# Products with zeros behind the attention products of slots 11 to 17

## The chip, the cores and the metric

The program runs on one NeuronCore of a Trainium2 chip. A core has five engines with queues of their own, which work at the same time and wait for each other by semaphores: TensorE (PE in the rows; its weight loads stand there as PEld), VectorE (DVE), ScalarE (ACT), GpSimd (POOL) and SyncE (SP, which here only issues transfers). TensorE writes into eight banks of PSUM; VectorE and ScalarE read them. The metric is the time of one execution on the device in microseconds (us); lower is better.

## The reference

Three stages, each on the result of the one before. For the attention there are 2 batches of 8 heads, 768 positions and a width of 64; a query sees the keys less than 16 positions away and 24 block summaries.

```python
scores_l = scale * np.matmul(q, k.transpose(0, 1, 3, 2))        # kept where |i - j| < 16
scores_s = scale * np.einsum('bhsd,bhnd->bhsn', q, k_sum) + np.log(block)
a = softmax(concatenate([scores_l_m, scores_s]))
attn_out = a @ concatenate([v, v_sum])
...
expert_idx = argmax(x_normed @ emb_normed.T / tau)               # 1536 rows, 8 experts, one each
out[mask] = gate * (relu(x[mask] @ w1[e]) @ w2[e])
...
h = x @ w_in                                                     # 512 -> 2048
return (h * cos(h)) @ w_out
```

## The kernel before, in words

**Attention in slots.** Two heads of one batch are a pair; there are 8 pairs, and each is done in two halves, so there are 16 half-pairs. The loop `for i in range(NH + 2)` runs over 18 slots, i = 0 to 17, and works as a pipeline of three half-pairs. Slot i does, in this order on TensorE:

- transposes for the pair to come: `pk` (line 205) in even slots, `pq` (line 178) in odd ones;
- the scores of half-pair i, `ps` (line 263; 12 products);
- the output products of half-pair i-2, `po` (`attn_av`, line 307; 12 products of a 120-row `aT` with the values and a column of ones), into a PSUM tile named `po` of which there is one;
- the transposes of half-pair i-1, `pa` (line 291; 6).

VectorE adds the mask to the scores (line 272), takes the maxima (279), and turns `po` into output rows (lines 313, 314, 316: add, reciprocal, multiply). ScalarE copies `pa` to `aT` (line 296) and takes the exponentials (284). So from one slot to the next there is a chain: `po`, then `pa` on TensorE, then the copy `aT` on ScalarE, then the next slot's `po`. That `po` also needs line 316 of the slot before, which frees the one tile. Slots 16 and 17 have no scores and no preparation.

**What else stands in the last slots.** The string `PLAN` places pieces of the routing of batch 0 in the slots 4 to 17: norms, logits, the pick of the expert, positions, and from slot 13 the scattering of its rows to DRAM by GpSimd (line 542). When the rows have landed, window 0 of the experts is loaded from there (line 751), scaled by its gate (764), transposed (`px`, line 778, behind slot 17's `po`), copied by ScalarE (780) and VectorE (781), and the first products of the experts (`h`, line 720) begin.

**The first expert window.** It forms `h`, then `y` (both line 720, 128 rows); in between stand turns of `h` (`pz`, line 851), the two halves of the transposes of window 1 (`px`, line 787, copied in lines 789 and 790), and the routing of batch 1 (transposes `pxr`, line 374, copied in 377; sums of squares in line 406). The weights of all windows are split into two parts by ScalarE (629) and VectorE (630). Windows 1 to 6 follow, then the dense stage; every product there is line 720 too.

**What sets the order.** The attention's own code is under `manual_schedule()`: it stays in the order in which it is written. What is written later, the expert stage and the routing of batch 1, is placed by the framework's scheduler, by its own estimate of when each engine is free; it can put such an instruction between those of the last slots. On the chip each engine then works through its list in that order.

**Zeros.** `still` is a tile of zeros [128, 256] in SBUF. `keep_warm` (line 1010) multiplies it with itself into an unused bank, three times in the first 18 us (line 1013).

Of the kernel before, what the change touches and what calls it, by code (L numbers as in the profile page):

```python
# [21 lines left out]
P = 128  # L22
# [29 lines left out]
ON_VECTOR = "e2 k4 k6 k8 k12 k14 x2 x3 x5"  # L52

EARLY = (2, 12)
NWMAX = 24
TT = 384
TWO_PI = 2.0 * math.pi
# [47 lines left out]
def fused_kernel(ctx, tc, q, k, v, emb, tau, w1, w2, w_in, w_out, consts, out):  # L105
    nc = tc.nc
# [57 lines left out]
    def shuffle(raw, n, scale, ap, eng, r=None):  # L164

        if r is None:
            r = ap.tile([P, QJ, 2, D], F32, tag="shuf", name="shuf", bufs=1)
        r = r[0:n]
        eng.tensor_scalar(
            r.rearrange("p j h d -> p h j d"), raw.rearrange("p h (j d) -> p h j d", d=D),  # L170
            scale, 1.0, op0=ALU.mult, op1=ALU.mult,
        )
        return r
# [52 lines left out]
    def prep_v1(bf, ap, eng):  # L226
        v4 = bf["vn"].rearrange("p h (j d) -> p h j d", d=D)
        va = ap.tile([QP, 2, 4, D], F32, tag="va", name="va", bufs=1)
        eng.tensor_tensor(va, v4[:, :, 0:4, :], v4[:, :, 4:8, :], op=ALU.add)
        eng.tensor_tensor(va[:, :, 0:2, :], va[:, :, 0:2, :], va[:, :, 2:4, :], op=ALU.add)  # L230
        eng.tensor_tensor(va[:, :, 0, :], va[:, :, 0, :], va[:, :, 1, :], op=ALU.add)
        return va
# [63 lines left out]
            nc.scalar.activation(aT[0:KC], pa[0:KC], AF.Copy)  # L296
        return aT

    def attn_av(g, half, aT, bf, xb, ps_s, ap):

        vw = bf["vw"][half]
        pb = ps_s.tile([P, 512], F32, tag="po", name="po")
        po = pb[:, 0:NU * (D + 1)].rearrange("p (u h d) -> p u h d", u=NU // 2, h=2)
        for u in range(NU):
            m = 64 * (u % 2)
            for hh in range(2):
                nc.tensor.matmul(
                    po[m:m + 64, u // 2, hh, :],
                    lhsT=aT[0:KC, (3 * hh + u // 2) * P + m:(3 * hh + u // 2) * P + m + 64], rhs=vw[0:KC, hh, u, :],
                    start=True, stop=True,  # L310
                )
        rs = ap.tile([P, NU // 2, 2], F32, tag="rs", name="rs")
        nc.vector.tensor_scalar(rs, po[:, :, :, D], 1e-9, None, op0=ALU.add)
        nc.vector.reciprocal(rs, rs)
        j0 = half * (NU // 2)
        nc.vector.tensor_tensor(
            xb[:, j0:j0 + NU // 2, 2 * g * D:2 * (g + 1) * D].rearrange(
                "p u (h d) -> p u h d", h=2
            ),
            po[:, :, :, 0:D], rs.unsqueeze(3).to_broadcast([P, NU // 2, 2, D]), op=ALU.mult,  # L320
        )
# [670 lines left out]
    with ExitStack() as actx:  # L992
        actx.enter_context(tc.manual_schedule())
        ap1 = actx.enter_context(tc.tile_pool(name="ap1", bufs=1))
        ap = actx.enter_context(tc.tile_pool(name="ap", bufs=2))
        ps_t = actx.enter_context(tc.tile_pool(name="ps_t", bufs=1, space=PSUM))
        ps_s = actx.enter_context(tc.tile_pool(name="ps_s", bufs=1, space=PSUM))
# [9 lines left out]
        still = ap1.tile([P, 2 * P], F32, name="still")  # L1007
# [10 lines left out]
        sets = []  # L1018
# [29 lines left out]
        def q_room():  # L1048
            r = xp.tile([P, 2 * ROW], F32, tag="xw", name="qr", bufs=3)
            return r[:, 0:2 * QJ * D].rearrange("p (j h d) -> p j h d", j=QJ, h=2)  # L1050
# [29 lines left out]
        xbs = []  # L1080
        x0p = actx.enter_context(tc.tile_pool(name="x0p", bufs=1, side="right"))
        for b in range(B):
            if b == 0:
                xb = x0p.tile([P, NU, ROW], F32, name="xb0")
            else:
                xb = big[:, 0:NU * ROW].rearrange("p (u r) -> p u r", u=NU)
# [4 lines left out]
        def moe_start():  # L1091
            for i in range(3):
                expert_slots(slots, wtis[0], i)
            slots.load(4)
            yield
            xws.append(load_x0())
            yield
            slots.load(8)
            for i in range(1, 3):
                xws.append(load_x(wtis[0], i, xp, 3))  # L1100
            yield
            for n in range(12):
                slots.convert(n + 1)
                yield
# [8 lines left out]
        ss, aTs = {}, {}  # L1113
# [3 lines left out]
        start = moe_start()  # L1117
# [23 lines left out]
        for item in PLAN.split(";"):  # L1141
            where, *names = item.split()
            todo = plan.setdefault((int(where[:-1]), where[-1]), [])
            for name in names:
                name, _, times = name.partition("*")
                todo += [gens[name]] * int(times or 1)

        def at(i, place):
            for piece in plan.get((i, place), ()):
                next(piece, None)  # L1150
# [7 lines left out]
        for i in range(NH + 2):  # L1158
            def prep_qv():
                nonlocal qs, va  # L1160
                qs = shuffle(raw["qn"], QP, SCALE, ap, nc.gpsimd, q_room())
                va = prep_v1(raw, ap, nc.vector if f"v{i}" in on_vector else nc.gpsimd)
                if p + 2 < NPR:
                    load_raw(*pairs[p + 2], raw, "qv")

            p, odd = divmod(i, 2)
            if i == 3:
                nc.sync.dma_start(cst[:, P:], consts[:, P:C_VIND])
                next(setup)
                for b, xb in enumerate(xbs):  # L1170
                    nc.gpsimd.memset(xb[:, :, DM:ROW], 0.0)
                    nc.gpsimd.tensor_copy(
                        xb[:, :, DM:DM + 1],
                        csa[:, C_TOK - C_VIND + b * NU:C_TOK - C_VIND + (b + 1) * NU].unsqueeze(2),
                    )
            if i == 7:
                zt = xp.tile([P, ROW], F32, tag="junk", name="zt")
                nc.gpsimd.memset(zt[:, 0:DM], 0.0)
                nc.gpsimd.memset(zt[:, DM:ROW], 1e6)
                for r0 in (S, NTOK):  # L1180
                    nc.sync.dma_start(
                        xs[r0:r0 + WT].rearrange("(a p) d -> p a d", p=P),
                        zt.unsqueeze(1).to_broadcast([P, WT // P, ROW]),
                    )
            at(i, "0")
            nx = sets[(p + 1) % 2] if p + 1 < NPR else None
            if nx is not None and not odd and i > 2:
                pk = ps_t.tile([P, QJ, P], F32, tag="tr", name="pk")
                prep_k(
                    nx, kr, [pk], ap, nc.vector if f"k{i}" in on_vector else nc.gpsimd,  # L1190
                    f"e{i}" in on_vector,
                )
            elif nx is not None and odd and i > 1:
                prep_q(nx, qs, ps_t, nc.scalar)
            at(i, "p")
            if i in EARLY:
                prep_qv()
            if i < NH:
                s, nmx, vsm = attn_scores(
                    odd, sets[p % 2], ps_s, ap, va if nx is not None and odd and i > 1 else None  # L1200
                )
                ss[i] = s
            at(i, "s")
            if i == 0:
                prep_v3(sets[0], means_v(va))
                va = prep_v1(raw, ap, nc.gpsimd)
                load_raw(*pairs[2], raw, "v")
                load_vw(*pairs[1], 0, sets[1]["vw"][0])
            if i == 1:
                prep_q(nx, qs1, ps_t, nc.scalar)  # L1210
            if i == 2:
                pk = ps_t.tile([P, QJ, P], F32, tag="tr", name="pk")
                prep_k(nx, kr, [pk], ap, nc.gpsimd, f"e{i}" in on_vector)
            at(i, "c")
            if i >= 2:
                b, g = pairs[p - 1]
                attn_av(g, odd, aTs.pop(i - 2), sets[(p - 1) % 2], xbs[b], ps_s, ap)
                if p + 1 < NPR:
                    load_vw(*pairs[p + 1], odd, nx["vw"][odd])
            at(i, "h")  # L1220
            if 0 <= i - 1 < NH:
                aTs[i - 1] = attn_aT(ss.pop(i - 1), ps_a, ap, i)
            if i == 1:
                keep_warm(4, P, ps_s, "s")
            if i < NH:
                attn_exp(s, nmx)
            if nx is not None and not odd and i and i not in EARLY:
                prep_qv()
            if odd and p + 2 < NPR:
                kr = shuffle(raw["kn"], QP + 4, 1.0, ap, nc.vector if i == 1 else nc.gpsimd)  # L1230
                if p + 3 < NPR:
                    load_raw(*pairs[p + 3], raw, "k")
            if i == 1:
                vsm1 = means_v(va)
                load_vw(*pairs[1], 1, sets[1]["vw"][1])
            if i == 2:
                prep_v3(sets[1], vsm1)
            elif nx is not None and odd and i > 1:
                prep_v3(nx, vsm)
            at(i, "e")  # L1240
            if i == 0:
                prep_k(nx, kr, two_banks(), ap, nc.gpsimd)
# [119 lines left out]

    n_all = nc.values_load(wtis[1][0:1, 2:3], min_val=0, max_val=NWMAX)
    with tc.For_i(NSLOT, n_all, 1) as it, ExitStack() as lctx:
# [74 lines left out]
```

## Time and profile before

| | us |
|---|---|
| median of 3 runs | 539.42 (539.02 to 539.49) |
| profiled execution: time | 539.12 |
| profiled execution: span of the program | 537.3 |
| TensorE busy | 506.7 (94%) |
| VectorE busy | 404.3 (75%) |
| ScalarE busy | 304.0 (57%) |
| GpSimd busy | 107.6 (20%) |
| mean granted clock of TensorE | 0.984 of full speed |

The attention takes the first 96 us, the experts run from about 98 to 266 us, the dense stage from there. Busy shares are means over stages with different limits; the clock's mean of 0.984 comes from a start at half speed and one stretch in the attention. Times in rows are microseconds from the start of the span unless they are marked ns. TensorE's products of 32-bit numbers stand as two rows each (x24 for 12 products), transposes as one.

### The profile page before, as it was taken

The numbers are of one execution on the slowest core, as the hardware profiler recorded it, in microseconds if no ns is written. First come the engines' busy times: TensorE is split into PE (matmuls) and PEld (weight loads), VectorE is DVE, ScalarE is ACT, GpSimd is POOL, SyncE is SP. The second block draws the span as 40 slices with busy tenths as digits, with TensorE's granted clock in tenths as the row PEclk, the third lists the DMA queues.
The fourth block names the chain that finished last, engine by engine and source line by source line (L and its number), as shares of the span: only waits on it lengthen the run. The fifth ranks groups of instructions, "written<-read, shape, count | busy, mean of one in ns | idle before, by whom it ended". The sixth has DMA issues, their size and how long they took to land. (4 is left out here: it accounts for less than half of the span.)

```text
span 537.3 us, 10198 instructions
## 1 busy us (share of the span) xinstructions
PE 506.7 (94%) x3748; PEld 459.7 (86%) x3748; DVE 404.3 (75%) x834; ACT 304.0 (57%) x642; POOL 107.6 (20%) x134
## 2 busy tenths in 40 slices
PE   7879977899999999999999999999999999999993
PEld 6657656679999999999999999999999999999992
DVE  5689784898768688889779998976699765655562
ACT  2778865997656556566557675633364433333330
POOL 3787574751534000000000000000000000001222
PEclk9999986999999999999999999999999999999998
DMA  8999747787797566766304433220010000001111
GB/s 213 243 206 253 176 109 254 266 285 244 247 333 259 160 209 219 234 197 199 119 2 137 138 117 119 78 79 0 1 40 2 1 0 1 0 2 59 60 59 63
DMA packets 47688, 72.31 MB, mean 135 GB/s; under 512 B 21256, under 2 KB 21512, under 8 KB 47632
## 3 DMA queue, kind: packets, MB, share of 16 engines
q1 hardware_dynamic: 44800, 62.11, 39.6%
q0 software_dynamic: 2832, 9.49, 5.0%
q8 instruction: 31, 0.51, 0.4%
q14 instruction: 25, 0.20, 0.1%
HBM read 64.22 MB, written 7.37 MB: 133 GB/s over the span
## 5 line engine op out<-in xcount | busy, mean ns | idle before, releaser
L720 PE MATMUL po<-sl,gt 128*128 128x512 f32 x567 | 139.8, 391 | 0.0
L720 PEld LDWEIGHTS po<-sl,gt 128*128 128x128 f32 x567 | 105.5, 188 | 18.2
L720 PE MATMUL ph<-yT,sl 128*128 128x384 f32 x576 | 107.7, 336 | 0.0
L720 PEld LDWEIGHTS ph<-yT,sl 128*128 128x128 f32 x576 | 101.2, 188 | 3.7
L630 DVE TENSOR_TENSOR sl<-raw,sl 128x512 fp32r<-128x512 f32 x112 | 75.0, 706 | 11.3 <-ACT sl L629 10.9
L973 POOL DMA_INDIRECT out_dram<-acc,perm x12 | 12.0, 998 | 345.1 <-DVE acc L1349 342.6
L720 PE MATMUL py<-ht,sl 128*128 128x256 f32 x576 | 73.8, 284 | 0.0
L629 ACT ACTIVATE sl<-raw 128x512 fp32r<-128x512 f32 x112 | 63.5, 625 | 17.5 <-PE py L720 12.3
L720 PE MATMUL ph<-xT,sl 128*128 128x256 f32 x576 | 72.3, 282 | 1.0 <-DVE ht L816 1.0
L720 PEld LDWEIGHTS ph<-xT,sl 128*128 128x128 f32 x576 | 69.7, 188 | 2.4 <-DVE ht L816 1.4
L720 PEld LDWEIGHTS py<-ht,sl 128*128 128x128 f32 x576 | 70.4, 188 | 0.9 <-issue 0.6
L930 ACT ACTIVATE u<-u 128x384 f32<-128x384 f32 x64 | 33.6, 525 | 62.9 <-DVE u L929 62.8
L934 ACT ACTIVATE gt<-t 128x384 fp32r<-128x384 f32 x63 | 33.0, 524 | 31.3 <-DVE t L933 31.1
L926 ACT ACTIVATE t<-ph 128x384 f32<-128x384 f32 x64 | 31.3, 488 | 31.6 <-PE ph L720 31.2
L933 DVE TENSOR_TENSOR t<-ph,u 128x384 f32<-128x384 f32 (+1 forms) x66 | 35.8, 544 | 17.7 <-ACT u L930 17.5
L935 DVE TENSOR_TENSOR gt<-t,gt 128x384 fp32r<-128x384 f32 x63 | 35.1, 557 | 17.2 <-ACT gt L934 16.6
L928 DVE TENSOR_SCALAR u<-t 128x384 f32<-128x384 f32 x64 | 23.0, 359 | 27.7 <-ACT t L926 27.2
L929 DVE TENSOR_TENSOR u<-t,u 128x384 f32<-128x384 f32 x64 | 35.6, 557 | 1.1
L720 PE MATMUL ph<-yT,early 128*128 128x384 f32 x192 | 36.1, 338 | 0.2 <-DVE yT L1296 0.2
L720 PEld LDWEIGHTS ph<-yT,early 128*128 128x128 f32 x192 | 33.9, 188 | 1.7 <-DVE yT L1296 0.5
L284 ACT ACTIVATE s<-s,nmx 128x120 f32<-128x120 f32 x96 | 29.0, 385 | 2.6 <-DVE nmx L279 1.5
L815 ACT ACTIVATE ht<-ph 128x256 fp32r<-128x256 f32 x48 | 17.8, 378 | 15.9 <-PE ph L720 15.9
(189 smaller groups left out, 652.8 us busy)
## 6 DMA issues: line engine op xcount, KB each, us to landing
raw<-in_moe_w_dram SPq DMA_DIRECT2D x56, 512.0 KB, 4.1
raw<-in_moe_w_in_dram SPq DMA_DIRECT2D x16, 512.0 KB, 3.7
raw<-in_moe_w_out_dram SPq DMA_DIRECT2D x16, 512.0 KB
vw<-in_v_dram SPq DMA_DIRECT2D x32, 120.0 KB, 6.1
xw<-xs POOLq DMA_DIRECT2D x6, 516.0 KB
kn<-in_k_dram SPq DMA_DIRECT2D x8, 384.0 KB, 4.6
qn<-in_q_dram SPq DMA_DIRECT2D x8, 384.0 KB, 5.0
vn<-in_v_dram SPq DMA_DIRECT2D x8, 384.0 KB, 5.8
```

What stands on the lines that cost most here:

```text
L284: nc.scalar.activation(s[:, u, :], s[:, u, :], AF.Exp, bias=nmx[:, u:u + 1])
L629: nc.scalar.activation(sl[:, 0, c], r, AF.Copy)
L630: nc.vector.tensor_tensor(sl[:, 1, c], r, sl[:, 0, c].bitcast(F32), op=ALU.subtract)
L720: nc.tensor.matmul(acc, lhsT=lw(a), rhs=lx(c), start=(first and i == 0), stop=(last and i == 2))
L815: nc.scalar.activation(ht[:, 0], ph, AF.Relu)
L926: nc.scalar.activation(t, ph, AF.Copy, scale=1.0 / TWO_PI, bias=0.25)
L928: nc.vector.tensor_scalar(u, t, ROUND, -ROUND, op0=ALU.add, op1=ALU.add)
L929: nc.vector.tensor_tensor(u, t, u, op=ALU.subtract)
L930: nc.scalar.activation(u, u, AF.Sin, scale=TURN)
L933: nc.vector.tensor_tensor(g, ph[:, cs], u[:, cs], op=ALU.mult)
L934: nc.scalar.activation(gt[:, 0], g, AF.Copy)
L935: lo = nc.vector.tensor_tensor(gt[:, 1], g, gt[:, 0].bitcast(F32), op=ALU.subtract)
```

## The change

A table `FILL` gives the slots 11 to 17 a number of extra products. `attn_av` issues them behind its own twelve: zeros (128x128) times zeros (128x112), into columns 400 to 511 of the bank in which `po` uses the columns 0 to 389. Nobody reads these columns. All slots together get 34 such products.

```diff
+FILL = {11: 4, 12: 4, 13: 4, 14: 5, 15: 5, 16: 6, 17: 6}
...
-    def attn_av(g, half, aT, bf, xb, ps_s, ap):
+    def attn_av(g, half, aT, bf, xb, ps_s, ap, fill=0):
...
                     start=True, stop=True,
                 )
+
+        for _ in range(fill):
+            nc.tensor.matmul(
+                pb[:, 400:512], lhsT=still[:, 0:P], rhs=still[:, 0:112], start=True, stop=True
+            )
         rs = ap.tile([P, NU // 2, 2], F32, tag="rs", name="rs")
...
-                attn_av(g, odd, aTs.pop(i - 2), sets[(p - 1) % 2], xbs[b], ps_s, ap)
+                attn_av(
+                    g, odd, aTs.pop(i - 2), sets[(p - 1) % 2], xbs[b], ps_s, ap, FILL.get(i, 0)
+                )
```

In the built program line 313 of VectorE (320 after), the first reader of `po`, waits for the last instruction that wrote the tile: before, the last of the twelve products; now, in the slots 11 to 17, the last product with zeros.

The change also moves what the scheduler places. TensorE from slot 16 to the first expert products, before (lines of before):

```order
L307 MATMUL po<-vw_129,aT 64x65 x12
L291 MATMUL pa<-cst,s 120x128 x6
L374 MATMUL pxr<-cst,big 128x128
L307 MATMUL po<-vw_130,aT 64x65 x12
L778 MATMUL px<-cst,xw 128x128 x4
L374 MATMUL pxr<-cst,big 128x128 x4
L720 MATMUL h<-sl,xT 128x512 x18
```

and now (lines of the changed kernel, which are 2 higher up to line 311 and 7 higher behind the new loop at 315; 381 is 374, 785 is 778):

```order
L309 MATMUL po<-vw_129,aT 64x65 x12
L316 MATMUL po<-still 128x112 x6
L293 MATMUL pa<-cst,s 120x128 x6
L381 MATMUL pxr<-cst,big 128x128
L309 MATMUL po<-vw_130,aT 64x65 x12
L316 MATMUL po<-still 128x112 x6
L785 MATMUL px<-cst,xw 128x128 x4
L381 MATMUL pxr<-cst,big 128x128 x4
L727 MATMUL h<-sl,xT 128x512 x18
```

Here only the products with zeros are new: they stand between `po` and `pa`, and in slot 17 between `po` and the transposes of the first expert window.

ScalarE at the same place, before (`sl` is a weight tile, `junk` takes the squares for batch 1's norms, `hr` is the first half of `h`):

```order
L629 ACTIVATE sl<-raw 128x512
L377 ACTIVATE big<-pxr 128x512
L406 ACTIVATE junk,nm_91<-big 128x512
L780 ACTIVATE xT<-px 128x4x128
L629 ACTIVATE sl<-raw 128x512 x7
L377 ACTIVATE big<-pxr 128x512
L844 ACTIVATE hr<-h 128x512
L406 ACTIVATE junk,nm_91<-big 128x512
```

and now (636 is 629, 384 is 377, 413 is 406, 787 is 780, 851 is 844):

```order
L636 ACTIVATE sl<-raw 128x512
L384 ACTIVATE big<-pxr 128x512
L413 ACTIVATE junk,nm_91<-big 128x512 x3
L787 ACTIVATE xT<-px 128x4x128
L636 ACTIVATE sl<-raw 128x512 x7
L384 ACTIVATE big<-pxr 128x512
L851 ACTIVATE hr<-h 128x512
```

Two more sums of squares have moved in front of the copy of the first window's transposes.

TensorE in the `y` products of the first window, before (`px` of line 787 are the transposes of window 1):

```order
L720 MATMUL y<-sl,ht 128x512 x2
L787 MATMUL px<-cst,xw 128x128 x3
L720 MATMUL y<-sl,ht 128x512 x6
L787 MATMUL px<-cst,xw 128x128
L374 MATMUL pxr<-cst,big 128x128
L851 MATMUL pz<-cst,hr 128x128 x4
L720 MATMUL y<-sl,ht 128x512 x6
L787 MATMUL px<-cst,xw 128x128 x4
L720 MATMUL y<-sl,ht 128x512 x6
L374 MATMUL pxr<-cst,big 128x128 x2
L720 MATMUL y<-sl,ht 128x512 x4
L720 MATMUL ph<-xT,sl 128x256 x18
```

and now (727 is 720, 794 is 787, 858 is 851):

```order
L727 MATMUL y<-sl,ht 128x512 x8
L794 MATMUL px<-cst,xw 128x128
L858 MATMUL pz<-cst,hr 128x128 x4
L727 MATMUL y<-sl,ht 128x512 x4
L794 MATMUL px<-cst,xw 128x128 x3
L727 MATMUL y<-sl,ht 128x512 x12
L794 MATMUL px<-cst,xw 128x128 x4
L381 MATMUL pxr<-cst,big 128x128 x4
L727 MATMUL ph<-xT,sl 128x256 x3
L858 MATMUL pz<-cst,yr 128x128 x3
L727 MATMUL ph<-xT,sl 128x256 x17
```

The second half of window 1's transposes stood ten `y` products ahead of window 1's first products (`ph`, which read them); it now stands behind the last `y` product, directly ahead of `ph`.

## Rows read from the trace of the kernel before

**Rows 1.** The page, part 2: clock granted to TensorE in 40 slices of 13.4 us, tenths.

```profile
PEclk9999986999999999999999999999999999999998
```

**Rows 2.** Windows: length, busy us (instructions) of PE, PEld, DVE, ACT, POOL; clock; DMA share; GB/s.

```profile
52.00:55.00 3.00, 2.45 (x38) 2.14 (x38) 2.87 (x6) 2.73 (x7) 0.00 (x0) 1.00 1.02 191
...
76.00:77.00 1.00, 0.00 (x0) 0.00 (x0) 0.93 (x6) 1.00 (x5) 0.63 (x1) 0.50 0.00 0
89.00:90.00 1.00, 1.00 (x27) 0.95 (x24) 0.74 (x1) 1.00 (x5) 0.58 (x1) 0.71 0.05 20
...
160.00:170.00 10.00, 10.00 (x87) 10.00 (x86) 8.12 (x13) 7.05 (x15) 3.90 (x5) 1.00 0.82 281
```

**Rows 3.** Timeline of PE, 15 to 18 us: start, length, instruction; the last use of zeros.

```profile
16.30 1.10 PE L1013 MATMUL pw<-still 128*128 128x128 f32 x8
```

**Rows 4.** Timeline of PE, slots 12 and 13; in brackets idle time before, and its end.

```profile
70.27 0.97 PE L307 MATMUL po<-vw,aT 120*64 120x65 f32 x24 [0.96 <-ACT aT L296]
...
73.08 0.85 PE L178 MATMUL pq<-cst,qr 96*128 96x96 f32 x8 [0.78 <-ACT kb L196]
...
77.17 1.59 PE L307 MATMUL po<-vw,aT 120*64 120x65 f32 x24 [2.13 <-ACT s L284]
```

**Rows 5.** Timeline of PE, slot 14 from its middle to the first expert product.

```profile
85.10 1.15 PE L307 MATMUL po<-vw,aT 120*64 120x65 f32 x13 [0.46 <-issue]
86.18 1.54 PE L291 MATMUL pa<-cst,s 128*120 128x128 f32 x6
87.64 1.48 PE L263 MATMUL ps<-kb,qT 64*64 64x120 f32 x24
89.05 1.20 PE L307 MATMUL po<-vw,aT 120*64 120x65 f32 x24
...
92.25 0.94 PE L307 MATMUL po<-vw,aT 120*64 120x65 f32 x24 [1.09 <-ACT s L284]
93.12 0.87 PE L291 MATMUL pa<-cst,s 128*120 128x128 f32 x6
...
94.94 0.94 PE L307 MATMUL po<-vw,aT 120*64 120x65 f32 x24 [0.34 <-issue]
...
97.98 4.81 PE L720 MATMUL h<-sl,xT 128*128 128x512 f32 x18 [1.08 <-DVE xT L781]
```

**Rows 6.** Timeline of all engines in the same stretch: VectorE, GpSimd and ScalarE.

```profile
85.36 0.91 DVE L272 TENSOR_TENSOR s<-ps,csa 128x720 f32<-128x720 f32 x1 [3.70 <-remote]
...
89.42 1.65 POOL L248 TENSOR_SCALAR vw<-vsm 24x768 f32<-24x768 f32 x2 [5.42 <-ACT s L284]
...
91.09 0.81 ACT L296 ACTIVATE aT<-pa 120x768 f32<-120x768 f32 x1 [0.82 <-PE pa L291]
...
94.03 0.81 ACT L296 ACTIVATE aT<-pa 120x768 f32<-120x768 f32 x1 [0.42 <-PE pa L291]
...
95.73 0.63 ACT L406 ACTIVATE junk<-big 128x512 f32<-128x512 f32 x1
...
96.55 0.60 ACT L780 ACTIVATE xT<-px 128x512 fp32r<-128x512 f32 x1
...
97.23 0.69 DVE L781 TENSOR_TENSOR xT<-px,xT 128x512 fp32r<-128x512 f32 x1 [0.26 <-ACT xT L780]
```

**Rows 7.** Timeline, the second half of window 1's transposes, to window 1's first products.

```profile
109.07 0.63 PE L787 MATMUL px<-cst,xw 128*128 128x128 f32 x4
...
110.79 0.58 ACT L789 ACTIVATE xT<-px 128x512 fp32r<-128x512 f32 x1
...
111.41 0.69 DVE L790 TENSOR_TENSOR xT<-px,xT 128x512 fp32r<-128x512 f32 x1
...
112.66 2.48 PE L720 MATMUL ph<-xT,sl 128*128 128x256 f32 x18
```

**Rows 8.** Timeline of PE, 49 to 57 us: transposes of batch 0's routing.

```profile
51.85 1.09 PE L374 MATMUL pxa<-cst,xb 128*128 128x128 f32 x8
52.78 0.60 PE L374 MATMUL pxr<-cst,xb 128*128 128x128 f32 x4
```

## The prediction

> **What bounds the kernel now.** I began with the page's row of granted clocks. It is full but for three places: the start, one stretch in the attention, and the end, when TensorE has finished [rows 1]. The windows narrow the stretch: the clock is at 0.50 (1.2 GHz) from 76 us, and in the window from 89 to 90 us it comes back, with a mean of 0.71 [rows 2]. So some 13.6 us of attention, slots 13 to 15, run at the lower level. Behind them TensorE is the bound: from 160 to 170 us both its products and its weight loads are busy for all of 10 us [rows 2], and it stays so until near the end. There is little slack there to absorb a later start, so I carry a shift of the expert stage into the end in full. The question is therefore when the first expert product starts, now at 97.98 [rows 5], and how long the first expert windows last.
>
> Next I read the timeline of TensorE in these slots, for who ends its waits. Slot 13's `po` starts at 77.17 after 2.13 us of idleness [rows 4]. Line 313 of slot 12 stands on VectorE behind the routing pieces of the plan, so that wait is VectorE's, and the clock has nothing to do with it. In slot 14 `po` pauses; at 85.10 its last 13 instructions go, and at 85.36 VectorE's add of the slot's scores starts, after 3.70 us in which the trace shows no engine that held it ("remote") [rows 5, 6]. From 85.10 the chain `po`, `pa`, copy, next `po` has little air: in slots 15 and 16 ScalarE waits for `pa` before each copy, 0.82 and 0.42 us [rows 6]. In slot 17 the chain goes on through the transposes, ScalarE's copy at 96.55, VectorE's at 97.23, and `h` at 97.98 [rows 5, 6].
>
> **The change, part by part.** *Price of a product.* The last use of zeros, four products of 128 columns at full clock, shows eight instructions in 1.10 us [rows 3]. Eight transposes take 1.09 and four 0.60 [rows 8], so one is 0.12 and 0.11 comes once, at the end; the same split gives the zeros 0.12 an instruction and about 0.235 a product. Now it has 112 columns, but its two weight loads keep 128. Bounds: 0.21 (112/128 of it) and 0.235. I take the upper one, as the loads do not shrink: 0.94 for four, 1.17 for five, 1.41 for six.
>
> *Slots 11 and 12: hidden.* Before slot 12's `po` TensorE idles 0.96 us, and before the `pq` at 73.08 it idles 0.78 [rows 4]. Slot 11's 0.94 fits the first gap, slot 12's the second but for 0.2, and `pq` leads to nothing that line 313 of slot 12 waits for. Without that cover each would cost 0.94. In exchange `pa` of slot 12 moves towards the idle stretch ahead of 76 us.
>
> *The clock.* Slot 12's products and the moved `pa` put more work ahead of the point where the clock fell, and slot 13's follow directly on its `po`. Transposes seem to hold it as well: around 52 us eight and then four stand back to back, 1.69 us of their own in a window with 2.45 us busy, at a clock of 1.00 [rows 2, 8]. So I expect it to hold, and if it does not the time is 546.6 (first rival). The Trainium skill, "TensorE: Matmul & The Clock Gate", Part 4 (PE-mode transpose), says that transposes do not count as busy for the clock in the way products do. By that rule the moved `pa` would help little, the clock would still fall, and the sum would be the rival's; the window around 52 us leans against it without refuting it.
>
> *Slot 13: hidden.* At full clock `po`, four products and `pa` take 0.87 + 0.94 + 0.87 from 77.17, to 79.85. (0.87 is the distance from one start to the next in slot 16 [rows 5].) Then comes the pause, which I leave as it is: nothing in the rows ties its end to TensorE's speed.
>
> *Slot 14.* From 85.10: the rest of `po` took 1.08 until `pa` started; at full clock half, 0.54. Then 1.17 of zeros and 0.87 for `pa`: 87.68, against 86.18 + 1.54 = 87.72 before [rows 5]. Clock and zeros cancel. `ps` is 0.65 shorter (1.48 at the half level), and the copy of 0.81 behind `pa` [rows 6] now decides: slot 15's `po` starts at about 88.55, 0.5 earlier.
>
> *Slots 15 to 17: not hidden.* Slot 15: 88.55 + 0.87 + 1.17 + 0.87 = 91.46; the copy starts at 91.5 (before 91.09), and slot 16's `po` at about 92.35 (before 92.25). Slot 16: 92.35 + 0.87 + 1.41 + 0.87 = 95.5; the copy starts at 95.54 (before 94.03), and `po` of slot 17 follows 0.91 later as before, at 96.45 (before 94.94): 1.5 late. VectorE's line 313 also waits for the last zero, but the path through `pa` and the copy is the longer one.
>
> *Slot 17 and the squares.* From `po` to line 780 it was 96.55 - 94.94 = 1.61; with six products more, the transposes are ready for ScalarE at 96.45 + 1.61 + 1.41 = 99.47. ScalarE has three sums of squares ahead of line 780 now. One took 0.82 (95.73 to 96.55), and the first began 1.70 after the copy of slot 17 started [rows 6]; so they end at 95.54 + 1.70 + 2.46 = 99.7. Line 780 is 3.15 late, and so is `h`: about 101.1. Without the zeros the squares alone would cost about 1.6 (two of 0.82).
>
> *The first expert window.* Before, window 1's second transposes ran at 109.07 and their copies ended at 112.10, ahead of `ph` at 112.66 [rows 7]: hidden. Now they stand behind the last `y`, and `ph` waits for them: 0.63 + 0.58 + 0.69 and some latency, about 2.0 us. TensorE has a part of that covered: transposes for batch 1, three `ph`, three `pz`. What speaks for less is that two squares have left ScalarE's list and fewer pieces break the `y` products. Bounds 0 and 2.9 (the whole chain and one more square's length); I take 1.5, nearer the chain.
>
> *Sum.* Start of `h` +3.1 (half-clock gain, zeros and squares together), first window +1.5: +4.6 on the profiled execution's 539.12, 543.7. The median of the runs lies 0.3 above it, so 544.0. With the lower price of a product some 0.4 less.
>
> **The rivals.** *The clock falls all the same* (546.6). The gap before 77.17 stays, about 2 us, with nothing of TensorE in it [rows 4]. For: slot 13's zeros come behind the gap, and what slot 12's push towards it are transposes. Against: more work ahead of it than before. This is where the page's rule, above, would lead. Then a product costs 0.47 at half level. Slot 13's double price vanishes in the pause, but after 85.10 slot 14 takes 1.17 more for zeros and loses the half-level gains of 0.54 in `po`, 0.67 in `pa`; with 0.2 in slot 15 until the clock is back, that is 2.6 over the forecast.
>
> *Faster: the pause goes with the slow clock* (538.0). If the pause of slot 14 hangs on TensorE being at half speed, a fast TensorE ends it, and VectorE's add at 85.36 starts up to 3.70 earlier. The next limit is GpSimd's line 248, which writes the block values that slot 16's `po` reads, at 89.42, half done at 90.25 [rows 6]: slot 16 at 90.3 in place of 92.35, `h` at 99.05, +1.05. For faster, the new order must then give something back: two squares (1.6) out of ScalarE's list in the first window and eight transposes (0.9) from between the `y` products, 2.5 together, which makes -1.4 in all. It decides at slot 16: only if its `po` starts by 90.5 and `ph` does not wait for line 790. Against: the slots 16 and 17 keep their zeros, and VectorE's 3.70 end at an event no engine shows.
>
> *No change* (539.4): slots 15 to 17 end on something other than TensorE, and the squares fill a wait that was there anyway. Against: ScalarE's waits for `pa` in the rows.
>
> **How the numbers follow.** Forecast 0.57; the clock falls 0.20; faster 0.16; no change 0.07. A difference under 0.2% (1.1 us) is about what a measurement of this kernel cannot tell from none. Faster 0.16, same 0.07, slower 0.77. The range runs from 538.4, which leaves out the better part of the faster case, to 547.4, above the rival with the fallen clock, which leaves out that both the clock and the window's whole chain go wrong. The forecast's own range is 541.5 (window 0, cheaper products, less late squares) to 545.5 (window 2.9).
>
> **What would show it.** In the new profile: the granted clock at 1.00 from 76 to 89 us (step of the clock); slot 16's and 17's `po` near 92.4 and 96.4; three squares back to back ahead of line 787 (780 before), and `h` near 101; `ph` waiting for lines 796 and 797 (789 and 790); the same length from there to the end. The prediction is wrong if slot 16's `po` starts by 90.5, if `h` starts before 98, or if the first window is shorter by what `h` was late.

## The result and the profile after

The changed kernel takes 545.73 us (median of 4 runs, 544.55 to 546.95) against 539.41 us (539.02 to 539.49) of the kernel before, in runs on one chip: a ratio of 1.0118, 95% interval 1.0087 to 1.0149, or 6.3 us more. The forecast was 544.0 us. The profiled execution of the changed kernel is the longest of the four (546.95 us, span 545.3), 7.8 us above that of before.

Part 2 of the page, the granted clock in 40 slices (the row that answers to [rows 1]):

```profile
PEclk9999998999999999999999999999999999999998
```

The seventh slice has 8 where it had 6: there is less half level than before, but it isn't gone. (In the kernel before, the windows show 1.00 from the start to 50 us and 0.73 from 530 us on, so the mean of 0.984 comes from the one stretch and the end, not from the start.) The windows, with the columns of [rows 2], show where it went:

```profile
52.00:53.00 1.00, 0.19 (x1) 0.15 (x2) 0.00 (x0) 1.00 (x4) 0.68 (x2) 0.74 1.14 265
...
80.00:83.00 3.00, 3.00 (x18) 2.66 (x20) 1.95 (x9) 0.18 (x2) 2.39 (x3) 0.50 0.90 270
84.00:86.00 2.00, 0.84 (x12) 0.60 (x11) 0.00 (x0) 1.50 (x6) 1.26 (x2) 1.00 0.80 202
87.00:90.00 3.00, 3.00 (x22) 2.88 (x20) 1.69 (x2) 0.00 (x0) 0.07 (x1) 0.50 0.90 348
```

In place of one stretch of 13.7 us from 76 us the records of the granted clock hold three of 3.4 us each: from 52.5 us, ahead of every added product, from 79.8 us and from 86.6 us. The timeline of TensorE from slot 13 to the first expert product shows what they met (columns as in [rows 4, 5]):

```profile
79.61 1.92 PE L316 MATMUL po<-still 128*128 128x112 f32 x8
81.33 1.49 PE L293 MATMUL pa<-cst,s 128*120 128x128 f32 x6
...
86.59 1.15 PE L309 MATMUL po<-vw,aT 120*64 120x65 f32 x13 [0.52 <-issue]
87.67 2.48 PE L316 MATMUL po<-still 128*128 128x112 f32 x10
89.94 0.87 PE L293 MATMUL pa<-cst,s 128*120 128x128 f32 x6
...
91.70 0.97 PE L309 MATMUL po<-vw,aT 120*64 120x65 f32 x24
92.60 1.37 PE L316 MATMUL po<-still 128*128 128x112 f32 x10
...
95.57 0.94 PE L309 MATMUL po<-vw,aT 120*64 120x65 f32 x24 [0.84 <-ACT aT L298]
96.44 1.59 PE L316 MATMUL po<-still 128*128 128x112 f32 x12
...
99.64 0.94 PE L309 MATMUL po<-vw,aT 120*64 120x65 f32 x24 [0.20 <-POOL xw L771]
100.50 1.59 PE L316 MATMUL po<-still 128*128 128x112 f32 x12
...
104.05 1.20 PE L727 MATMUL h<-sl,xT 128*128 128x512 f32 x4 [1.08 <-DVE xT L788]
```

Ten instructions with zeros take 1.37 us at full clock and twelve 1.59, so 0.11 for one more instruction and 0.22 for a product; slot 14's ten stand in the half level and take 2.48. The same stretch on VectorE and ScalarE (answers to [rows 6]):

```profile
86.87 0.91 DVE L274 TENSOR_TENSOR s<-ps,csa 128x720 f32<-128x720 f32 x1 [3.56 <-remote]
...
98.72 0.81 ACT L298 ACTIVATE aT<-pa 120x768 f32<-120x768 f32 x1 [1.55 <-PE pa L293]
...
101.94 0.63 ACT L413 ACTIVATE junk<-big 128x512 f32<-128x512 f32 x1
...
102.62 0.60 ACT L787 ACTIVATE xT<-px 128x512 fp32r<-128x512 f32 x1
```

Slot 14's pause is there again (3.56 us against 3.70), and this time TensorE's clock is full in it, as the window from 84 to 86 us shows. Now the first expert window, TensorE's timeline from window 1's first products (answers to the last row of [rows 7]):

```profile
119.14 0.62 PE L727 MATMUL ph<-xT,sl 128*128 128x256 f32 x3 [0.25 <-ACT xT L796]
...
119.94 2.25 PE L727 MATMUL ph<-xT,sl 128*128 128x256 f32 x17
122.12 0.83 PE L393 MATMUL pl<-big,enT 128*32 128x384 f32 x2
122.88 0.39 PE L727 MATMUL ph<-xT,sl 128*128 128x256 f32 x1
123.19 0.83 PE L393 MATMUL pl<-big,enT 128*32 128x384 f32 x2
123.96 0.38 PE L727 MATMUL ph<-xT,sl 128*128 128x256 f32 x1
...
125.35 0.83 PE L393 MATMUL pl<-big,enT 128*32 128x384 f32 x2
126.11 0.51 PE L727 MATMUL ph<-xT,sl 128*128 128x256 f32 x2
```

`pl` are the logit products of batch 1's routing, four for each half (two rows each). The four of the first half stand one by one between products of window 1, and the stretch from 122.12 to 126.11 holds only them and three `ph`: 3.99 us.

Laid end to end, the start times of the two timelines say where the profiled execution lost its time. (Slot 14's rest is its second part of `po`, behind the pause; "dense" is the first product of the dense stage, at 262.44 and 270.70 us; slot 11's `po` starts at 65.42 and 66.98 us.)

| stretch | before | changed | difference | forecast |
|---|---|---|---|---|
| start to slot 11 | 65.42 | 66.98 | +1.56 | 0 |
| slot 11 to slot 14's rest | 19.68 | 19.61 | -0.07 | 0 |
| slot 14's rest to slot 15 | 3.95 | 5.11 | +1.16 | -0.50 |
| slot 15 to 16 | 3.20 | 3.87 | +0.67 | +0.60 |
| slot 16 to 17 | 2.69 | 4.07 | +1.38 | +1.41 |
| slot 17 to `h` | 3.04 | 4.41 | +1.37 | +1.61 |
| `h` to dense | 164.46 | 166.65 | +2.19 | +1.5 |

The first and the last line of the table rest on these rows, before:

```profile
65.42 0.97 PE L307 MATMUL po<-vw,aT 120*64 120x65 f32 x24
...
262.44 1.38 PE L720 MATMUL ph<-yT,early 128*128 128x384 f32 x7
```

and now:

```profile
66.98 0.97 PE L309 MATMUL po<-vw,aT 120*64 120x65 f32 x24
...
270.70 1.38 PE L727 MATMUL ph<-yT,early 128*128 128x384 f32 x7
```

Behind that both run alike (265.78 and 265.73 us to TensorE's last product). The differences add up to 8.3 us in this one pair of executions, 2 us more than the medians differ. The 1.56 us ahead of slot 11, and so ahead of the first added product, were not put there by these products: TensorE waited 1.41 us for GpSimd at 52.81 us, where it had waited 0.21, and then ran at half level.

### The profile page after: what moved, and what is told of

Its sections match the earlier page's. It is cut to its first block, busy times and chain, and to the rows that moved or that the text cites. A ratio compares the mean times of both kernels' runs of the same rounds, so it can differ in the third digit from the quotient of the medians.

```text
span 545.3 us, 10338 instructions
## 1 busy us (share of the span) xinstructions
PE 516.0 (95%) x3816; PEld 468.8 (86%) x3816; DVE 403.2 (74%) x834; ACT 304.7 (56%) x642; POOL 106.5 (20%) x134
## 5 line engine op out<-in xcount | busy, mean ns | idle before, releaser
L637 DVE TENSOR_TENSOR sl<-raw,sl 128x512 fp32r<-128x512 f32 x112 | 73.8, 693 | 13.3 <-ACT sl L636 12.9
```

The lines of the kernel that those rows point to most:

```text
L637: nc.vector.tensor_tensor(sl[:, 1, c], r, sl[:, 0, c].bitcast(F32), op=ALU.subtract)
```

## Experiments

Three theories stood against each other at first: A, the zeros of the slots 14 to 17 lie on the chain and the order of the first window adds something; B, the new order alone costs the time; C, short stretches at half clock do. Every run's time is compared with runs of the kernel before on the same chip. There the kernel before spread more (534.0 to 542.4 us in the runs that the ratios use; medians of 538.5, 538.1 and 538.2 in three groups, each on a chip of its own) than in the runs above, so each ratio has its interval. One table for all, with the stretches from each kernel's one profiled execution, and the time at half level between 50 and 105 us:

| kernel | ratio (95%) | 11 to 17 | 17 to `h` | `h` to dense | half level |
|---|---|---|---|---|---|
| before | | 29.52 | 3.04 | 164.46 | 13.7 |
| changed | 1.0118 (1.0087 to 1.0149) | 32.66 | 4.41 | 166.65 | 10.2 |
| zeros up to 16 | 1.0050 (1.0023 to 1.0077) | 31.07 | 3.04 | 163.45 | 3.4 |
| zeros in 17 | 1.0067 (1.0041 to 1.0093) | 30.00 | 4.42 | 165.17 | 10.2 |
| zeros in 11 to 13 | 0.9970 (0.9945 to 0.9996) | 28.99 | 3.04 | 162.44 | 3.4 |
| zeros in 14 to 16 | 1.0033 (1.0004 to 1.0062) | 33.21 | 3.05 | 163.45 | 13.7 |
| changed, `pl` a block | 1.0053 (1.0030 to 1.0076) | 29.96 | 4.42 | 164.60 | 0 |
| before, `pl` broken up | 1.0097 (1.0060 to 1.0134) | 26.62 | 3.04 | 166.25 | 6.8 |
| transposes in 11 to 13 | 1.0023 (0.9993 to 1.0053) | 29.36 | 4.15 | 162.51 | 13.7 |
| before, scatters late | one run, 539.76 us | 24.92 | 8.40 | 164.48 | 10.2 |
| before, scatters split | 1.0044 (1.0022 to 1.0066) | 29.43 | 3.05 | 164.95 | 6.8 |
| split, zeros in 11 to 13 | 1.0034 (1.0008 to 1.0060) | 29.16 | 4.16 | 165.25 | 10.2 |
| before, `pl` in one quarter | 1.0133 (1.0081 to 1.0184) | 28.82 | 3.04 | 171.35 | 6.8 |

**The change in parts.** Four kernels differ from the changed one in the table alone:

```diff
-FILL = {11: 4, 12: 4, 13: 4, 14: 5, 15: 5, 16: 6, 17: 6}
+FILL = {11: 4, 12: 4, 13: 4, 14: 5, 15: 5, 16: 6}    # zeros up to 16
+FILL = {17: 6}                                       # zeros in 17
+FILL = {11: 4, 12: 4, 13: 4}                         # zeros in 11 to 13
+FILL = {14: 5, 15: 5, 16: 6}                         # zeros in 14 to 16
```

> The zeros of slots 11 to 16 stay (4, 4, 4, 5, 5, 6), those of slot 17 go; with that the scheduler places the expert stage as in the kernel before (one square ahead of the copy, second transposes of window 1 between the y products). Theory A (zeros of slots 14 to 16 lie on the chain, slot 17's zeros and the new order make the rest): slot 17's po at about 96.5 to 98, h 1.5 to 3 us later than before, the same length behind it, so +1.5 to +3 us. Theory B (the new order alone makes the loss): within 1 us of before. Theory C (short stretches at half clock make the loss, and the zeros of slots 11 to 13 bring them): +4 to +6 us, as in the changed kernel.

> Only slot 17's six zeros stay; they alone bring the new order (three squares ahead of the copy, second transposes of window 1 behind the last y). Up to slot 17's po all as before, po at about 95. Theory A: squares and zeros make h 3.1 us late, the first window adds 0 to 1.5: +3 to +4.5 us. Theory B (order alone): +5 to +6, the whole loss. Theory C (half clock): 0 to +1.5 us, with the half-clock stretch as in the kernel before.

> Only the zeros of slots 11 to 13 stay (4 each); order of the expert stage as before. Theory A: they are hidden behind VectorE's plan work, so slot 14's last products start at 85.1 to 85.5; the clock is full or half for shorter than 13.6 us, which gives slot 14 up to 1.2 us: -1.2 to +0.5 us. Theory B: the same as A. Theory C: the clock falls in short stretches, ahead of slot 11 too, and costs 1.5 to 3 us: +1.5 to +3 us.

> Only the zeros of slots 14 to 16 stay (5, 5, 6); order of the expert stage as before. The clock falls at 76 as before, so slot 14's zeros run at half level. Theory A: slot 14 +2 us, slots 15 and 16 +1.1 and +1.4 less the waits there: h 2.5 to 4 us late, +2.5 to +4 us. Theory B (order alone): within 1 us. Theory C (half clock brought by slots 11 to 13): within 1.5 us, since those slots have no zeros.

Zeros up to 16 cost 0.50% (2.7 us), inside A; B lies outside the interval of 1.2 to 4.1 us, and C, which begins at 4, only touches its end. Its timeline of TensorE gives the three slots without a fallen clock:

```profile
85.83 0.70 PE L309 MATMUL po<-vw,aT 120*64 120x65 f32 x13 [1.20 <-issue]
86.46 1.37 PE L316 MATMUL po<-still 128*128 128x112 f32 x10
...
89.39 0.97 PE L309 MATMUL po<-vw,aT 120*64 120x65 f32 x24
...
93.25 0.94 PE L309 MATMUL po<-vw,aT 120*64 120x65 f32 x24 [0.84 <-ACT aT L298]
...
97.32 0.94 PE L309 MATMUL po<-vw,aT 120*64 120x65 f32 x24 [0.20 <-issue]
```

From slot to slot 3.56, 3.86 and 4.07 us: the forecast's 3.45, 3.80 and 4.10. In the same kernel the logit products stay together; four of them take 0.78 us to the next `ph`, about what one took above (0.76):

```profile
118.18 0.85 PE L393 MATMUL pl<-big,enT 128*32 128x384 f32 x8 [0.46 <-ACT big L384]
...
118.96 1.10 PE L727 MATMUL ph<-xT,sl 128*128 128x256 f32 x7
```

Zeros in 17 alone cost 0.67% (3.6 us), inside A; the interval of 2.2 to 5.0 us leaves out C and touches the lower end of B. Slot 17 takes 1.38 us more to `h`, and the first window is in the changed kernel's order, with `pl` broken up. The two parts add up to the whole, within their intervals: 0.50% and 0.67% against 1.18%.

Zeros in 11 to 13 cost nothing: 0.30% less (1.6 us, a little below A's range), with an interval that ends at -0.04%. That is against C. Zeros in 14 to 16 cost 0.33% (0.2 to 3.3 us), a little below A's range and not apart from B's 1 us by its interval; its trace has the chain 3.7 us longer, slot 14's zeros at half level (2.48 us) among it. That profiled execution is still only 2.0 us above that of before, because slot 11 started 0.69 us earlier and `h` to dense was 1.01 us shorter, in places that these zeros don't touch: there one pair of profiles differs by a microsecond or so by itself.

**The order of the first window.** The table's last column but one has two kinds of kernels: with `pl` broken up `h` to dense took 166.65, 165.17 and 166.25 us, with a block of four in four quarters 162.44 to 165.25. These touch, since later windows vary too. The shorter stretch from window 1's first `ph` to window 2's first transposes (`px`) holds the two groups of `pl` and keeps the kinds apart: 25.95, 26.17 and 25.48 us broken up, 22.66 to 23.20 us as a block. Its end before and in the changed kernel (the starts are 112.66 and 119.14):

```profile
135.32 0.60 PE L787 MATMUL px<-cst,xw 128*128 128x128 f32 x4
```

```profile
145.09 0.60 PE L794 MATMUL px<-cst,xw 128*128 128x128 f32 x4
```

Two kernels take this apart (their A and B are new ones):

```diff
     pl = ps_r.tile([P, 512], F32, tag="r", name="pl")
-    for c in range(4):
-        nc.tensor.matmul(pl[32 * c:32 * (c + 1), 0:3 * P], ...)
+    with tc.high_priority(offset=100):    # the changed kernel, pl a block
+    with tc.high_priority(offset=-50):    # the kernel before, pl broken up
+        for c in range(4):
+            nc.tensor.matmul(pl[32 * c:32 * (c + 1), 0:3 * P], ...)
```

> The changed kernel with all its zeros; only the four logit products of batch 1's first half (pl, 32 columns each into a quarter of the partitions) are given a higher priority, so that they stand as a block and not one by one between products of window 1 (ph). In the changed kernel's trace the stretch from the first broken-up pl to the last takes 3.99 us where a block and as many ph take about 1.4. Theory A (the broken-up block is the order's cost): 2 to 2.6 us less than the changed kernel, so about +3.5 to +4.5 us against before. Theory B (the forecast's: ph waits for the moved transposes and copies of window 1): no gain, +6 us; ph keeps its wait and pl costs the same.

> The kernel before, without zeros; only batch 1's logit products have a lower priority, so that the four of the first half stand one by one between products (py) and the work around them moves back by some twenty products. Theory A: +2 to +2.6 us, and the group of pl grows from 1.7 to over 4 us of busy time. Theory B (the order of pl does not matter): within 0.8 us.

The changed kernel with a block costs 0.53% in place of 1.18%, some 3.5 us less by the two ratios (1.4 to 5.6 by their intervals); that is A, the point above its 2 to 2.6 us, and 2.9 us over the kernel before where 3.5 to 4.5 were expected. The ratios can't give all of it to `pl`: in the profiles the stretch from slot 11 to 17, with the same instructions, is 2.70 us shorter, at full clock and without slot 14's pause. What belongs to the block is the stretch from `ph` to `px`: 23.08 us in place of 25.95. The block's TensorE shows the forecast's own wait too, 1.66 us where the changed kernel had 0.25:

```profile
116.84 0.62 PE L728 MATMUL ph<-xT,sl 128*128 128x256 f32 x3 [1.66 <-ACT xT L797]
...
118.05 0.85 PE L394 MATMUL pl<-big,enT 128*32 128x384 f32 x8
```

Here ScalarE's copy of the late transposes stood behind two weight pieces that had waited 1.64 us for their transfer.

The other way round, the kernel before with `pl` broken up has the longer group (window 97 to 170 us; busy time, mean ns of one, idle time before):

```profile
L387 PE MATMUL pl<-big,enT 128*32 128x384 f32 x16 | 4.2, 498 | 0.0
```

In the kernel before it is

```profile
L386 PE MATMUL pl<-big,enT 128*32 128x384 f32 x16 | 1.7, 498 | 0.0
```

The kernel's time grows by 0.97% (3.2 to 7.2 us), more than the 2.5 us of the group; it also moves batch 1's logits back by 30 to 35 products, and what the rest comes from stays open.

Why is a block short? `pl` is 32 columns wide and each of the four writes a quarter of the partitions. One kernel keeps the block, and the time between its products, but sums all four into one quarter (the small operations behind it are fitted to that):

```diff
-    pl[32 * c:32 * (c + 1), 0:3 * P], ..., start=True, stop=True,
+    pl[0:32, 0:3 * P], ..., start=(c == 0), stop=(c == 3),    # batch 1 only
```

> The kernel before; batch 1's logit products (pl) stay a block of four, but all four sum into the same 32 partitions, one after the other, in place of a quarter each. If a block is short because its four products run side by side in quarters of the array: each of the two blocks takes about 3 us in place of 0.85, and batch 1 costs +3.5 to +4.5 us. If it is short because nothing stands between them: no change, within 0.8 us.

```profile
115.53 2.77 PE L388 MATMUL pl<-big,enT 128*32 128x384 f32 x8
118.23 1.20 PE L725 MATMUL ph<-xT,sl 128*128 128x256 f32 x8
```

2.70 us from the block's start to the next product, in place of 0.78, and 26.98 us from `ph` to `px`: here the four ran side by side only when they went to different quarters and nothing stood between. Twice 1.92 is the 3.8 us that were expected; the kernel lost 1.33% (4.4 to 9.9 us), with a wait of 2.42 us for window 2's transposed rows behind it, so the later routing cost something of its own. The Trainium skill, "TensorEngine Tiling (Array Packing)", Key Properties, says that tiles of the array work in parallel and that a change of the tiling mode drains TensorE. The first half agrees with the 0.78 against 2.70 us. For the second, a `pl` alone in the changed kernel took 0.76 us to the next `ph` and that `ph` 0.31 to the next `pl`; `ph` in a row are 0.13 apart (the seventeen from 119.94 to 122.12), so 0.18 us more for such a `ph` is an estimate of what a drain could be here; no run takes it apart.

**The clock and the transposes.** The forecast took transposes to hold the clock as products do:

```diff
-            nc.tensor.matmul(
-                pb[:, 400:512], lhsT=still[:, 0:P], rhs=still[:, 0:112], start=True, stop=True
-            )
+            nc.tensor.transpose(pb[:, 400:512], still[0:112, 0:P], ident[0:112, 0:112])
...
+FILL = {11: 8, 12: 8, 13: 8}
```

> Slots 11 to 13 get eight transposes of zeros each in place of four products with zeros (the same eight instructions in a row, same time); slots 14 to 17 nothing. If transposes hold the clock as products do (the forecast's reading): at most 7 us at half level between 70 and 92 us, like the runs with products in these slots (3.4, 3.4 and 6.8 us), time -2 to +0.5 us. If they do not count: 10 to 14 us at half level there, as in the runs without zeros in these slots (13.7, 13.7 and 10.2 us), time -0.5 to +1 us.

The clock stayed at 1.00 until 88.9 us and then was 0.50 for 13.7 us, into the first expert products. Within 70 to 92 us that is 3.1 us, so the clock was full where it had fallen before; the whole is as long as without them. The fall lies inside a wait of 4.30 us in slot 16, 2.7 us after its start:

```profile
90.51 1.62 PE L309 MATMUL po<-vw,aT 120*64 120x65 f32 x24 [4.30 <-POOL vw L250]
```

One profile doesn't settle it, and with a ratio from -0.07% to +0.53% neither does the time (its middle, +1.2 us, is above both expected ranges). The clock of every run says more. The mean granted clock was 0.978 in the ten runs with transposes, against 0.979 in the runs of the kernel before beside them. With products in the slots 11 to 13 it rose: to 0.985 (zeros up to 16) and 0.986 (11 to 13 alone) against 0.981 before, and to 0.990 (all the zeros, `pl` a block) against 0.979; with zeros in 17 alone and in 14 to 16 alone it stayed at 0.981. The split scatters below are the weakest case, 0.980 with these products and 0.978 without. The rule that the prediction cites from the Trainium skill, "TensorE: Matmul & The Clock Gate", Part 4 (PE-mode transpose), is that transposes do not count as busy in the way products do. The profile does not bear it out at 76 us; the mean clocks lean to it, with no gain to be seen from transposes, though up to 0.003 would be hidden by their scatter.

**The pause of slot 14.** In this run the pause isn't there at all: slot 14's `po` ran through, and slot 16's waited for GpSimd's block values. Two kernels move GpSimd's scatters (piece `Z`) to the place behind its writing of these values:

```diff
-    12h T*3 Z*6; ... 13h T*5 W;
+    12h T*3;     ... 13h T*5 W;13e Z*6;    # scatters late
+    12h T*3 Z*2; ... 13h T*5 W;13e Z*4;    # scatters split
```

> The kernel before; only the six scatters of GpSimd move behind its writing of the block values of the same slot (some 4 us later). If slot 14's pause hangs on the scatters: VectorE's add of slot 14 starts when the scores are there (by 83.5 us in place of 85.36), and a pause of like length stands in slot 14 or 15 until about 1.3 us after the last scatter; window 0 comes later, +2 to +5 us. If the pause hangs on something else in slot 14 (the clock among it): the add still starts at 85 to 86 us.

> The kernel before, no zeros; four of GpSimd's six scatters go behind its writing of the block values, two stay ahead of it. If TensorE's waits of slots 14 to 16 hang on GpSimd (the pause on the scatters, slot 16's products on the block values): the block values are written near 80 us in place of 89.42, the slots 14 to 17 run some 4 us shorter (as in the run with all six moved), window 0 is there about as early as there, and h starts 1 to 2 us earlier: -1 to -2.5 us. If the waits hang on something else: within 0.8 us.

> The same with the zeros of slots 11 to 13 (4 each). If these zeros are hidden and keep the clock up: 0 to 1.5 us less than the run with the split scatters alone. If they were only luck of the runs: the same within 0.8 us. If they lie on the chain now that GpSimd's waits are gone: +0.5 to +1 us over it.

With all six late slot 14 has no pause (VectorE's add at 81.19 us), against expectation no other slot has one, and 11 to 17 takes 24.92 us in place of 29.52, but window 0's rows come later and `h` waits for them: 8.40 us behind slot 17. Its one run, 1.7 us above the median of before, stays under the 2 to 5 us that were expected. This profile says little of the pause, though: it is of the second group, in which the three kernels with their scatters in place had none either. In the third group the kernel with its scatters in place (`pl` in one quarter) paused in slot 14 (3.71 us). With four late, in that group, the pause has moved to slot 15, on VectorE and ScalarE, around the last scatter:

```profile
87.12 0.97 POOL L542 DMA_INDIRECT xs<-xb,posi  x1 [0.30 <-issue]
...
87.51 0.16 DVE L313 TENSOR_SCALAR rs<-po 128x6 f32<-128x6 f32 x1 [2.19 <-remote]
...
89.06 0.81 ACT L296 ACTIVATE aT<-pa 120x768 f32<-120x768 f32 x1 [3.94 <-remote]
```

So the pause moved with the scatters, in one profile. TensorE's clock alone doesn't decide it: the changed kernel paused at full clock, and with `pl` broken up slot 14 ran at half level without a pause. But my expected gain of 1 to 2.5 us was wrong: the pause only changed its slot, `h` came 32.48 us behind slot 11 as before (32.56), and the runs took 0.44% more. Zeros in 11 to 13 on top made 0.1% less of it, inside what was expected if they are hidden, and not apart from nothing.

No run beats both kernels by more than zeros in 11 to 13 alone: 0.30% below before, 0.04% to 0.55% by its interval.

## Why the prediction was right, and where it was not

The direction, and 6.3 us in place of 4.6: the mechanism that was named (zeros on the chain from slot 14 on, hidden ahead of it) held, and two steps failed: the clock, and with it slot 14, and the wait in the first expert window.

*Price of a product.* 0.22 us at full clock, between the forecast's bounds of 0.21 and 0.235.

*Slots 11 to 13 hidden.* Right, by the run with these alone: from slot 11 to slot 13 its `po` take 11.75 us, as before.

*The clock.* Wrong as a step: it was to hold from 76 to 89 us, and 6.8 us of half level remained. The rival that it falls all the same was right in half. In the runs with products in slots 11 to 13 the half level between 50 and 105 us was 0 to 10.2 us, in those without 6.8 to 13.7: less on the whole, as the mean clock of all runs says too, but not at will, since stretches also came in places that no zeros touch (52.5 us in the changed kernel).

*Slot 14.* This is the term that was mis-sized: 0.50 less was forecast and 1.16 more measured, since slot 14's zeros met a half-level stretch (2.48 in place of 1.37 us). Where the clock held, in the run with zeros up to 16, the slot took 3.56 us, within 0.11 of the forecast.

*Slots 15 and 16.* +0.67 and +1.38 against +0.60 and +1.41, in the run up to 16 the same: right.

*Slot 17 and the squares.* +1.37 in the changed kernel and 1.38 with slot 17 alone, against 1.61. The three squares ran while TensorE was still at the zeros and the transposes: line 787 starts at 102.62, behind the last square, when the transposes of 101.93 are just done. So squares and zeros cover each other: they end within some 0.1 us, and the cost is that of one of them and not of both.

*The first expert window.* +1.5 was forecast, +2.19 measured, and the cause was another, so that the two are near each other is luck. `ph` was to wait for window 1's late transposes; it waited 0.25 us. The time went into `pl`, 4.2 us in place of 1.7. Up to window 2's first transposes the loss is 3.70 us, above the forecast's bound of 2.9; 1.5 us came back behind them, where the kernels with the order of before differ by up to 3.5 us. Of the 3.70 some 2.8 are accounted for: the 3.99 us from 122.12 on, where a block and three `ph` at 0.13 take about 1.2. The rest is open. The order of the changed kernel shows `pl` one by one between `ph`, right behind the rows that are quoted ahead of the prediction; I had followed the order to the first wait that I could name and not to the end of the stretch where the two orders differ.

*The rivals.* Faster, the pause going with the half-level clock: the pause stood at full clock, so its condition fell. Its second limit was real: in the three profiles without a pause (`pl` a block, `pl` broken up, transposes) slot 16 waited for the block values, which GpSimd begins to write at 89.6 to 91.1 us. No change: excluded by the interval.

## What to carry to other kernels

A filler instruction costs its length wherever the chain behind it has no wait to give, so give it only to slots whose next consumer waits for another engine; the same product was free in slots 11 to 13 and cost its full 0.22 us from slot 15 on. A few instructions ahead of a stretch that a scheduler places can change its order, and that may cost more than they do (here 2.5 against 1.4 us): compare the orders to the point where they agree again, and look for small products that had run side by side and now stand alone. Where the clock of one profile decides a term, take several profiles, compare the mean clock of all runs, or carry both levels in the range.

## What the runs showed of the hardware

Four products of 32 columns into four quarters of the partitions took 0.78 us as a block, 2.70 us into one quarter, and about 3.0 us one by one between full-width products. Around GpSimd's last scatters VectorE, and with four of them late ScalarE too, stopped for 2 to 4 us at an event that the trace puts down to none of the engines; with the scatters in their place this happened in 7 of 10 profiles, and the three without it are those of one group, on one chip. What decides it stays open. Stretches at half level came at different times from profile to profile, 3.4 to 13.7 us long, also ahead of everything that the kernels differ in. The runs of the unchanged kernel that the ratios use spread over 6.6 to 7.5 us within each group of experiments, where the four beside the changed kernel agreed within 0.5 us. In each group the longer runs tend to be those with the lower mean clock (0.969 to 0.991 in all; correlation -0.68 to -0.81): a line through them gives 2.8 to 3.8 us for 0.01 of the clock.
